# Another seven-product form for the second matrix product of an attention-and-GELU block

## The chip, the cores and the metric

The kernel runs on one core of a Trainium2 chip. The core has five engines with a queue of instructions each, worked through in order: TensorE (PE: matmuls, and PEld: the loads of their left sides), VectorE (DVE), ScalarE (ACT), GpSimd (POOL) and SyncE (SP, which only issues DMAs here). Engines wait for each other by semaphores. Matmul results lie in PSUM, in which the kernel holds eight tiles of 2 KB per partition (called banks here); everything else lies in SBUF. GpSimd does not read PSUM in this kernel.

The metric is the device time of one execution in microseconds. Before the change it is 203.3 us (median of three runs, 203.26 to 203.94).

## The reference

```python
# x: (8, 8, 512, 64), state: (8, 8, 32, 64): batches, heads, rows, depth
scores = scale * x @ state^T;   a  = softmax(scores);   xread = a  @ state
scores2 = scale * state @ x^T;  a2 = softmax(scores2);  sread = a2 @ x
rows = concatenate([xread, sread], axis=2)   # 8 batches of 512 + 32 rows, 512 wide
h = rows @ w_in                              # w_in: 512 x 2048
g = gelu(h)                                  # exact
out = g @ w_out                              # w_out: 2048 x 512, 4352 rows out
```

Inputs and output are float32; the kernel multiplies in bf16 and accumulates in float32.

## The kernel before, in words

For each of the eight batches the kernel makes the softmax weights `a`, folds the state into w_in (`P`, helpers `p_mm` and `p_all`), and gets g by `mm1`: two matmuls into a PSUM tile `hp` and one gelu on ScalarE, sixteen times per batch, written `M(k, k + 1)` for two of them. The 32 state rows of all batches together ("read-out") go through their own first product (`SR`) and second product (`R`).

The second product, g @ w_out, is plain for batch 0 (`mm2`). For batches 1 to 7 it is done in a seven-product form: g of a batch is cut into four quadrants `g_q(b, h, k)` (h: half of the rows, k: half of the 2048 inner columns), w_out into four quadrants `w_q[k][n]` (k: half of its rows, n: half of its columns). Seven products of quadrant size replace eight. Each left side is a quadrant of g or a sum of two (`g_sum`, one VectorE instruction of 128x2048 bf16, five per batch); each right side is a quadrant of w_out or a sum of two (`w_sums`, five in all, made once). A product is 16 matmuls (`x_mm`), and it accumulates in one of four banks `xp`. Products that share a bank are added there for free; the rest of the combination is done by `X` behind each product: per batch three bank copies on ScalarE, four adds on VectorE that read PSUM, and two subtractions on GpSimd (`u` and `v`, lines 658 and 622) of values in SBUF. The first product in a bank ("3" in bank 0) is copied before the second ("5") accumulates on it.

The order of the instructions is written out by hand; no scheduler moves them. From line 1171 on a loop runs over b, the batch whose g is being made, in eight slots p. Each slot begins with `M`, and most end with a product of batch b - 1. Slot 1 opens with the score matmuls of the next batch, slots 2 and 3 have its normalisation on VectorE (`norm`: a reduce, a reciprocal, a multiply), slot 5 has `p_all` (its matmuls use the banks of `xp` too) and then the first product of batch b itself, slot 7 the second. GpSimd rearranges the x of later batches (`rearr`, `rearr_ones`, lines 225 and 235) in slots 0, 5 and 7. SP's queue holds the output stores of the products (`x_out`) and the transposing DMAs of `xT` (slot 3) and `AT` (slot 5).

In the last pass (b = 7) slots 0 to 4 are `read_out_slot`: there the products of batch 6 stand between those of `SR`, which is a small seven-product form of its own, with adds on VectorE and ScalarE copies, in four PSUM tiles `sp` ("7" of it accumulates in the tile of "1", which VectorE reads in between). Slots 5 to 7 hold the products `R` of the read-out rows. Behind the loop come the products of batch 7, the last two of them in three pieces each (`l_mm`), so that adds and stores of the first pieces run beside the matmuls of the later ones.

The bank of each product, and the products that open one ("3" and "4" take a quadrant of g as it is):

```python
bank = {"3": 0, "4": 1, "5": 0, "2": 1, "1": 2, "6": 3, "7": 2}[name]
first = name in "3416"
```

Of the kernel before, what the change touches and what calls it, by code (L numbers as in the profile page):

```python
# [17 lines left out]
def kernel(  # L18
# [541 lines left out]
    w_sum = {}  # L560

    def w_add(name, x, y, op):
        if name == "3":
            pair = persist.tile([128, 2, MH, NH], BF16, name="ws_34", tag="mix0")
            w_sum["3"], w_sum["4"] = pair[:, 0], pair[:, 1]
        elif name != "4":
            tag = {"6": "mix1", "1": "mix2", "7": "mix3"}[name]
            w_sum[name] = persist.tile([128, MH, NH], BF16, name=f"ws_{name}", tag=tag)
        nc.vector.tensor_tensor(out=w_sum[name], in0=x, in1=y, op=op)

    def w_sums(i):
        (b11, b12), (b21, b22) = w_q
        w_add(*(
            ("3", b12, b22, ALU.subtract),
            ("4", b21, b11, ALU.subtract),
            ("6", b11, b12, ALU.add),
            ("1", b11, b22, ALU.add),
            ("7", b21, b22, ALU.add),
        )[i])
# [14 lines left out]
    def g_sum(b, name):  # L594
        (h0, k0), (h1, k1), op = G_SUMS[name]
        t = apool.tile([128, MH, 256], BF16, name="gsum", tag="gsum")
        nc.vector.tensor_tensor(out=t, in0=g_q(b, h0, k0), in1=g_q(b, h1, k1), op=op)  # L597
        xs[b, "g" + name] = t
# [20 lines left out]
    def c22(b):  # L619
        xs[b, "v"] = c_tile("v")  # L620
        o = xs[b, "o", 1]
        nc.gpsimd.tensor_tensor(  # L622
            out=xs[b, "v"], in0=xs[b, "q"], in1=o[:, :, :NH], op=ALU.subtract
        )
        if b < B - 2:
            c22_add(b)

    def c22_add(b):
        o = xs[b, "o", 1]
        nc.vector.tensor_tensor(out=o[:, :, NH:], in0=xs[b, 3], in1=xs[b, "v"], op=ALU.add)  # L630
        x_out(b, 1)

    def X(b, name):
        bank = {"3": 0, "4": 1, "5": 0, "2": 1, "1": 2, "6": 3, "7": 2}[name]
        first = name in "3416"
        if first:
            xs[b, bank] = otile([128, 2, NH], "xp", bank)
        ps = xs[b, bank]
        lhs = {"3": (0, 0), "4": (1, 1)}.get(name)
        lhs = xs[b, "g" + name] if lhs is None else g_q(b, *lhs)  # L640
        rhs = {"5": w_q[1][1], "2": w_q[0][0]}.get(name)
        rhs = w_sum[name] if rhs is None else rhs
        x_mm(ps, lhs, rhs, first)
        if name == "3":
            xs[b, "s3"] = c_tile("s3")
            if b > 1:
                nc.scalar.copy(out=xs[b, "s3"], in_=ps)
            for h in range(2):
                xs[b, "o", h] = hpool.tile([128, 2, d_model], FP32, name="oh", tag=f"oh{h}")
        elif name == "4":  # L650
            xs[b, "s34"] = c_tile("s34")
            nc.vector.tensor_tensor(out=xs[b, "s34"], in0=ps, in1=xs[b, "s3"], op=ALU.add)
        elif name == "5":
            o = xs[b, "o", 0][:, :, NH:]
            nc.scalar.copy(out=o, in_=ps)  # L655
            xs[b, "u"] = c_tile("u")
            x_out(b, 0, right)
            nc.gpsimd.tensor_tensor(out=xs[b, "u"], in0=xs[b, "s34"], in1=o, op=ALU.subtract)  # L658
        elif name == "2":
            nc.scalar.copy(out=xs[b, "o", 1][:, :, :NH], in_=ps)  # L660
            c22(b)
        elif name == "1":
            xs[b, "q"] = c_tile("q")
            nc.vector.tensor_tensor(out=xs[b, "q"], in0=ps, in1=xs[b, "s34"], op=ALU.add)
        elif name == "7":
            nc.vector.tensor_tensor(
                out=xs[b, "o", 0][:, :, :NH], in0=ps, in1=xs[b, "u"], op=ALU.add
            )
            x_out(b, 0, left)
# [8 lines left out]
    both = slice(0, 2)  # L678

    def L4():  # L680
        b = B - 1
        ps = xs[b, 1] = otile([128, 2, NH], "xp", 1)
        x_mm(ps, g_q(b, 1, 1), w_sum["4"], True)
        xs[b, "s34"] = c_tile("s34")
        nc.vector.tensor_tensor(out=xs[b, "s34"], in0=ps, in1=xs[b, "s3"], op=ALU.add)
        xs[b, "y"] = c_tile("q")
        nc.vector.tensor_tensor(out=xs[b, "y"], in0=xs[b, 3], in1=xs[b, "s34"], op=ALU.add)

    def L5():
        b = B - 1  # L690
        x_mm(xs[b, 0], xs[b, "g5"], w_q[1][1], False)
        nc.scalar.copy(out=xs[b, "o", 0][:, :, right], in_=xs[b, 0])
        rows_out(0, both, right, nc.sync)

    def L5_u():
        b = B - 1
        xs[b, "u"] = c_tile("u")
        nc.vector.tensor_tensor(
            out=xs[b, "u"], in0=xs[b, "s34"], in1=xs[b, "o", 0][:, :, right], op=ALU.subtract
        )  # L700

    def L2():
        b = B - 1
        x_mm(xs[b, 1], xs[b, "g2"], w_q[0][0], False)
        c21 = xs[b, "o", 1][:, :, left]
        nc.scalar.copy(out=c21, in_=xs[b, 1])
        rows_out(1, both, left, nc.sync)
        xs[b, "v"] = c_tile("v")
        nc.vector.tensor_tensor(out=xs[b, "v"], in0=xs[b, "y"], in1=c21, op=ALU.subtract)

    PIECES = ((0, 0, NH, 2), (1, 0, NH // 2, 0), (1, NH // 2, NH, 1))

    def l_mm(ps, name, j, n0, n1, first):
        for m in range(MH):
            nc.tensor.matmul(  # L715
                ps,
                lhsT=xs[B - 1, "g" + name][:, m, 128 * j:128 * j + 128],
                rhs=w_sum[name][:, m, n0:n1],
                start=(first and m == 0),
                stop=(m == MH - 1),  # L720
                skip_group_check=True,
            )

    def L1():
        b = B - 1
        for j, n0, n1, at in PIECES:
            ps = xs[b, "x", j, n0] = otile([128, n1 - n0], "xp", at)
            l_mm(ps, "1", j, n0, n1, True)
            nc.vector.tensor_tensor(
                out=xs[b, "o", 1][:, j, NH + n0:NH + n1],  # L730
                in0=ps,
                in1=xs[b, "v"][:, j, n0:n1],
                op=ALU.add,
            )
        rows_out(1, both, right, nc.sync)

    def L7():
        b = B - 1
        for j, n0, n1, at in PIECES:
            ps = xs[b, "x", j, n0]  # L740
            l_mm(ps, "7", j, n0, n1, False)
            nc.vector.tensor_tensor(
                out=xs[b, "o", 0][:, j, n0:n1], in0=ps, in1=xs[b, "u"][:, j, n0:n1], op=ALU.add
            )
            rows_out(0, slice(j, j + 1), slice(n0, n1), nc.scalar if n0 else nc.sync)
# [97 lines left out]
    def r_homes():  # L843
        pair = [att.tile([128, 2, MH, 128], BF16, name="rs", tag="xT") for _ in range(2)]
        one = att.tile([128, MH, 128], BF16, name="rs1", tag="AT")
        homes = [pair[0][:, 0], pair[0][:, 1], pair[1][:, 0], pair[1][:, 1], one]
        rs["homes"] = dict(zip("51267", homes))

    def r_sum(name):
        t = rs["g" + name] = rs["homes"][name]  # L850
        (h0, k0), (h1, k1), op = G_SUMS[name]
        nc.vector.tensor_tensor(out=t, in0=r_q(h0, k0), in1=r_q(h1, k1), op=op)
# [7 lines left out]
    def R(name):  # L860
# [4 lines left out]
        bank = {"3": 0, "4": 1, "5": 0, "2": 1, "1": 2, "6": 3, "7": 2}[name]  # L865
        first = name in "3416"
        if first:
            home = {"3": 1, "4": 2, "6": 2}
            rs[bank] = otile([128, NH], "rp", home[name]) if name in home else ftile([128, NH], "rp")
        ps = rs[bank]  # L870
        lhs = {"3": (0, 0), "4": (1, 1)}.get(name)
        lhs = rs["g" + name] if lhs is None else r_q(*lhs)
        rhs = {"5": w_q[1][1], "2": w_q[0][0]}.get(name)
        rhs = w_sum[name] if rhs is None else rhs
# [9 lines left out]
        add, sub = ALU.add, ALU.subtract  # L884
        if name == "3":
            nc.scalar.copy(out=c_new("s3"), in_=ps)
            for h in range(2):
                rs["o", h] = opool.tile([128, d_model], FP32, name="osb", tag="osb")
        elif name == "4":
            nc.vector.tensor_tensor(out=c_new("s34"), in0=ps, in1=rs["s3"], op=add)  # L890
        elif name == "5":
            o = rs["o", 0][:, NH:]
            nc.scalar.copy(out=o, in_=ps)
            nc.vector.tensor_tensor(out=c_new("u"), in0=rs["s34"], in1=o, op=sub)
        elif name == "1":
# [10 lines left out]
        elif name == "7":  # L906
            nc.vector.tensor_tensor(out=rs["o", 0][:, :NH], in0=ps, in1=rs["u"], op=add)
            r_out(0)
# [379 lines left out]
```

## Time and profile before

| what | us |
|---|---|
| median of three runs | 203.3 |
| profiled execution, whole time | 203.97 |
| its span, first to last instruction | 202.1 |
| TensorE matmul busy | 195.0 |
| VectorE busy | 155.9 |
| ScalarE busy | 139.2 |
| GpSimd busy | 67.3 |
| one product, 16 matmuls, in the chain | 1.75 |
| `g_sum` (L597), mean of 35 / median | 1.367 / 1.218 |
| add from PSUM, 128x512 float32 (L652, L664, L666, L630) | 0.68 to 0.69 |
| ScalarE bank copy, 128x512 (L647, L655, L660) | 0.59 |
| GpSimd `u` (L658), `v` (L622), mean | 1.47, 1.38 |

All durations are from one execution. The span is 1.87 us shorter than the whole time of that execution, and that execution is 0.67 us above the median. A timeline row has its start, its length, the engine and line, the operation with output and inputs, and in brackets the idle time of the engine before it and who ended it. Rows merged as x16 have the sum of their time. Lines are those of the program before.

### The profile page before, as it was taken

How to read it: one execution, taken by the hardware profiler on the slowest of the kernel's cores; microseconds unless marked ns; L12 is line 12 of the kernel's file. 1: busy time of each engine (PE TensorE's matmuls, PEld its weight loads, DVE VectorE, ACT ScalarE, POOL GpSimd, SP SyncE). 2: the span in 40 equal slices, each digit the busy share in tenths (PEclk: the TensorE clock that was granted, in tenths of full speed). 3: DMA queues.
4: the chain of work that ended last, by engine and by line, in shares of the span. 5: the costliest groups of instructions: out<-in, count | busy, mean ns of one | idle time of the engine just before them, and what ended most of it. 6: DMA issues, size and time to landing. Idle time of an engine off the chain costs nothing.

```text
span 202.1 us, 4900 instructions
## 1 busy us (share of the span) xinstructions
PE 195.0 (97%) x2030; PEld 134.4 (66%) x2035; DVE 155.9 (77%) x248; ACT 139.2 (69%) x251; POOL 67.3 (33%) x75
## 2 busy tenths in 40 slices
PE   7899999999999999999999999999999999999992
PEld 2434544465767677667767587677776878878892
DVE  2954875989996799986996967587758888894982
ACT  3785578798986878677967596688859477854020
POOL 8963503424259198431537202410220011200000
PEclk9999999999999999999999999999999999999999
DMA  6999999969665789592875208450107001040135
GB/s 195 196 171 203 205 199 194 181 140 158 89 116 107 208 96 156 116 133 78 107 156 148 63 2 112 146 114 0 52 27 184 3 0 55 0 159 0 52 105 159
DMA packets 40566, 23.16 MB, mean 115 GB/s; under 512 B 21856, under 2 KB 39136, under 8 KB 40544
## 3 DMA queue, kind: packets, MB, share of 16 engines
q0 software_dynamic: 13984, 8.10, 29.4%
q1 hardware_dynamic: 25872, 14.36, 29.3%
q10 hardware_dynamic: 688, 0.39, 0.6%
q8 instruction: 16, 0.26, 0.5%
q14 instruction: 6, 0.05, 0.1%
HBM read 17.30 MB, written 8.91 MB: 130 GB/s over the span
## 4 chain that ended last, share of the span: by engine, by line
PE 91%; DVE 5%; ACT 2%; issue 1%; ACTq 0%
PE xp L603 40%; PE hp L506 26%; PE op L548 5%; PE sp L810 3%; PE rp L876 3%; PE p_ps L441 2%; PE op L532 2%; PE xp L715 2%; PE pt L333 2%; PE warm_ps L150 2%; PE sr L917 1%; ACT P L955 1%; DVE gsum L597 1%; DVE P L955 1%; PE hp L1064 1%
## 5 line engine op out<-in xcount | busy, mean ns | idle before, releaser
L513 ACT ACTIVATE g<-hp 128x512 bf16<-128x512 f32 x124 | 65.9, 607 | 21.1 <-PE hp L506 14.8
L506 PE MATMUL hp<-AT,P 128*128 128x512 bf16 x248 | 61.2, 379 | 0.0
L603 PEld LDWEIGHTS <-gsum 128*128 128x128 bf16 x528 | 51.2, 98 | 11.4 <-DVE gsum L597 0.8
L597 DVE TENSOR_TENSOR gsum<-g 128x2048 bf16<-128x2048 bf16 x35 | 47.3, 1367 | 0.5
L506 PEld LDWEIGHTS <-P 128*128 128x128 bf16 x248 | 23.5, 98 | 20.6 <-issue 0.6
L603 PE MATMUL xp<-ws,gsum 128*128 128x256 bf16 x304 | 36.3, 273 | 0.4 <-DVE gsum L597 0.4
L603 PE MATMUL xp<-ws,g 128*128 128x256 bf16 x224 | 26.7, 272 | 0.3
L603 PE MATMUL xp<-w_out_bf,gsum 128*128 128x256 bf16 x224 | 26.6, 273 | 0.0
L603 PEld LDWEIGHTS <-g 128*128 128x128 bf16 x224 | 21.7, 98 | 5.3 <-issue 1.9
L658 POOL TENSOR_TENSOR u<-s,oh 128x512 f32<-128x512 f32 x6 | 8.8, 1468 | 40.1 <-ACT oh L655 40.1
L225 POOL COPY x<-xb 128x1024 bf16<-128x1024 bf16 x12 | 14.6, 1244 | 17.5 <-DMA xb<-in_x_dram 17.5
L622 POOL TENSOR_TENSOR v<-q,oh 128x512 f32<-128x512 f32 x6 | 8.3, 1379 | 19.5 <-ACT oh L660 17.2
L235 POOL COPY xo<-xb 128x1024 bf16<-128x1024 bf16 x12 | 12.1, 1041 | 5.0 <-PE sr L917 5.0
L955 ACT CAST P<-p_ps 128x512 bf16<-128x512 f32 x25 | 12.7, 606 | 0.1
L356 DVE TENSOR_TENSOR a<-e,ics 128x512 bf16<-128x512 bf16 x14 | 11.7, 834 | 0.5
L548 PE MATMUL op<-w_out_bf,g 128*128 128x512 bf16 x44 | 11.1, 380 | 0.5 <-issue 0.3
L955 DVE CAST P<-p_ps 128x512 bf16<-128x512 f32 x15 | 9.4, 684 | 1.7 <-PE p_ps L441 1.7
L353 DVE TENSOR_REDUCE cs<-e 128x16 f32<-128x512 bf16 x14 | 9.5, 677 | 0.9 <-ACT e L340 0.9
L441 PE MATMUL p_ps<-w_in_bf,sbd 64*32 64x512 bf16 x248 | 9.4, 380 | 0.0
L513 ACT ACT_TABLE_LOAD x7 | 9.0, 1283 | 0.1
L548 PEld LDWEIGHTS <-g 128*128 128x128 bf16 x48 | 4.2, 98 | 5.6 <-issue 0.8
L340 ACT ACT_TABLE_LOAD x6 | 7.7, 1283 | 0.1
(143 smaller groups left out, 240.7 us busy)
## 6 DMA issues: line engine op xcount, KB each, us to landing
out_dram<-oh SPq DMA_DIRECT2D x15, 256.0 KB, 2.5
xb<-in_x_dram POOLq DMA_DIRECT2D x7, 512.0 KB, 5.9
out_dram<-oh SPq DMA_DIRECT2D x6, 512.0 KB, 3.5
w_in_bf<-in_moe_w_in_dram POOLq DMA_DIRECT2D x6, 256.0 KB, 12.2
out_dram<-osb SPq DMA_DIRECT2D x5, 256.0 KB, 3.2
w_out_bf<-in_moe_w_out_dram POOLq DMA_DIRECT2D x4, 256.0 KB, 8.6
w_out_bf<-in_moe_w_out_dram POOLq DMA_DIRECT2D x2, 512.0 KB, 13.5
x0f<-in_x_dram SPq DMA_DIRECT2D x3, 256.0 KB, 3.9
```

The source lines that it names most:

```text
L225: nc.gpsimd.tensor_copy(out=A.x4[:, :, :, 64 * t:64 * t + 64].rearrange("p j c d -> p c j d"), in_=src[:, t],)
L235: eng.tensor_copy(out=A.xo[:, :, :, 2 + 64 * t:66 + 64 * t].rearrange("p j c d -> p c j d"), in_=src[:, t],)
L353: nc.vector.reduce_sum(out=cs, in_=e4, axis=AX.X)
L356: nc.vector.tensor_tensor(out=A.a[:, :, hs].rearrange("p g (c n) -> p g c n", n=NS), in0=e4, in1=ics[:, :, :].to_broadcast((128, G, 2, NS) ...
L441: nc.tensor.matmul(ps[t][32 * c:32 * c + 32, :], lhsT=sbd[64 * t:64 * t + 64, b, c, 32 * t:32 * t + 32], rhs=w_in_bf[64 * t:64 * t + 64, c ...
L506: nc.tensor.matmul(hp, lhsT=Ps[b][:, t, m * 128:(m + 1) * 128], rhs=atts[b].AT[:, :, t, :], start=(t == 0), stop=(t == 1),)
L513: nc.scalar.activation(out=gs[b][:, m, :], in_=hp, func=AF.Gelu)
L548: nc.tensor.matmul(ops[b, j], lhsT=gs[b][:, m, j * 128:(j + 1) * 128], rhs=w_out_bf[:, m, :], start=(m == 0), stop=(m == MC - 1),)
L597: nc.vector.tensor_tensor(out=t, in0=g_q(b, h0, k0), in1=g_q(b, h1, k1), op=op)
L603: nc.tensor.matmul(ps[:, j - js[0], :], lhsT=lhs[:, m, 128 * j:128 * j + 128], rhs=rhs[:, m, :], start=(first and j == js[0] and m == 0), ...
L658: nc.gpsimd.tensor_tensor(out=xs[b, "u"], in0=xs[b, "s34"], in1=o, op=ALU.subtract)
L955: copy(out=Ps[b][:, t, f * 512:(f + 1) * 512], in_=ps[t])
```

## The change

The seven products are those of another scheme. Its left sides are chained: "5" is a sum of two quadrants, "6" is "5" less a third, "3" is a quadrant less "6", and "7" is a difference by itself. So there are four sums per batch in place of five, and the products "1", "2" and "4" take quadrants as they are. The right sides are chained in the same way: four sums of w_out in place of five, `w_diff`. The products "1", "6" and "7" accumulate in one bank one after another, "5" and "3" in a second, "2" and "4" have one each. Per batch ScalarE copies four banks (`snap`: c2, c4, u, s5) and VectorE makes four adds, each of a bank and a copy; GpSimd has no part in it.

The order in the slots is new as well. Before: "4", "5", "1", "2" in slots 0 to 3, "7" in slot 5, and "3" and "6" of the batch itself in slots 5 and 7. After: "1", "6", "5", "7" in slots 0 to 3, "3" in slot 5, "2" and "4" of the batch itself in slots 5 and 7. The sums "5" and "6" are made together in slot 0, "7" in slot 2, "3" in slot 3. `sr_w`, which makes the sums for the read-out, moves from slot 0 to slot 1, behind product "6". In the read-out slots and in `R` the same scheme is used. Behind the loop the order is "1", "5" (in pieces), "6", `R("3")`, "7", "3" (in pieces); the lower half of the output rows of batch 7 leaves in one store of 512 KB after "7", the right half of the upper rows in three pieces after "3", where before there were stores of 256 KB after "5", "2" and "1" and three pieces after "7".

```diff
+    (b21, b22), (b11, b12) = w_q
+    def w_diff(name):
...
+        x, y = {
+            "5": (b12, b11),
+            "6": (b22, w_t.get("5")),
+            "7": (b22, b12),
+            "4": (b21, w_t.get("6")),
+        }[name]
+        nc.vector.tensor_tensor(out=w_t[name], in0=x, in1=y, op=ALU.subtract)
...
+    def chain(name, q, got):
+        a11, a12, a21, a22 = q(0, 1), q(0, 0), q(1, 1), q(1, 0)
+        return {
+            "1": (a11,),
+            "2": (a12,),
+            "4": (a22,),
+            "5": (a21, a22, ALU.add),
+            "6": (got.get("5"), a11, ALU.subtract),
+            "7": (a11, a21, ALU.subtract),
+            "3": (a12, got.get("6"), ALU.subtract),
+        }[name]
...
+    BANK = {"2": 0, "1": 1, "6": 1, "7": 1, "5": 2, "3": 2, "4": 3}
+
+    def add(out, x, y):
+        nc.vector.tensor_tensor(out=out, in0=x, in1=y, op=ALU.add)
+
+    def snap(b, name, tag, ps):
+        xs[b, name] = c_tile(tag)
+        nc.scalar.copy(out=xs[b, name], in_=ps)
...
+        x_mm(ps, x_lhs(b, name), w_rhs(name), first)
+        if name == "2":
             if b > 1:
-                nc.scalar.copy(out=xs[b, "s3"], in_=ps)
+                snap(b, "c2", "c2", ps)
+        elif name == "4":
+            snap(b, "c4", "c4", ps)
+        elif name == "1":
...
+            add(xs[b, "o", 0][:, :, left], ps, xs[b, "c2"])
+            x_out(b, 0, left)
+        elif name == "6":
+            snap(b, "u", "u", ps)
         elif name == "5":
...
+            snap(b, "s5", "s5", ps)
+        elif name == "7":
+            add(xs[b, "o", 1][:, :, right], ps, xs[b, "s5"])
+            add(xs[b, "o", 1][:, :, left], ps, xs[b, "c4"])
+            x_out(b, 1)
+        elif name == "3":
+            add(xs[b, "o", 0][:, :, right], ps, xs[b, "u"])
             x_out(b, 0, right)
-            nc.gpsimd.tensor_tensor(out=xs[b, "u"], in0=xs[b, "s34"], in1=o, op=ALU.subtract)
...
+            if p < 5 and nb < B:
                 if p == 0:
-                    g_sum(b - 1, "5")
-                    if b > 2:
-                        sr_w("5216"[b - 3])
-                X(b - 1, "45127"[p])
-                if p < 3:
-                    g_sum(b - 1, "127"[p])
+                    g_sum(b - 1, "56")
+                if p == 2:
+                    g_sum(b - 1, "7")
+                if p == 3:
+                    g_sum(b - 1, "3")
+                if p < 4:
+                    X(b - 1, "1657"[p])
+                if p == 1 and b > 2:
+                    sr_w("5216"[b - 3])
...
@@ read_out_slot
             SR("5", 1)
             SR("2", 1)
             SR_gelu("52", 1)
-            X(c, "2")
+            X(c, "7")
             SR("1", 1)
             SR("6", 1)
         if p == 4:
             M(k, k + 1)
             SR_gelu("6", 1)
             SR("7", 1)
             SR_gelu("7", 1)
-            c22_add(c)
-            X(c, "7")
+            X(c, "3")
...
             if p == 5:
-                X(b - 1, "7")
+                X(b - 1, "3")
...
-                g_sum(b, "6")
...
-                X(b, "3")
+                X(b, "2")
...
-                X(b, "6")
+                X(b, "4")
     b = B - 1
-    for name in "521":
-        g_sum(b, name)
-    L4()
-    g_sum(b, "7")
+    g_sum(b, "56")
+    X(b, "1")
+    g_sum(b, "73")
     L5()
-    L5_u()
-    L2()
-    R("7")
-    L1()
-    L7()
+    X(b, "6")
+    R("3")
+    X(b, "7")
+    L3()
```

## The prediction

> **What bounds the kernel now.** I read the page first, then the waits of TensorE, a table by stretch, and then the timeline at those places where the change puts a wait in front of TensorE. The page's chain that ended last, and the waits:
>
> ```profile
> span 202.1 us, 4900 instructions
> PE 195.0 (97%) x2030; PEld 134.4 (66%) x2035; DVE 155.9 (77%) x248; ACT 139.2 (69%) x251; POOL 67.3 (33%) x75
> PE 91%; DVE 5%; ACT 2%; issue 1%; ACTq 0%
> ...
> PE xp L603 <- DVE gsum L597: 0.4, 1, 0.4
> ...
> 42.00:198.00 156.00, 155.26 (x1660) 115.98 (x1657) 127.92 (x182) 110.76 (x201) 45.74 (x42) 1.00 0.46 93
> ```
>
> The reader should see that from 42 to 198 us, where all seven-product work lies, TensorE is busy 155.26 of 156.00 us at the full clock (the last line: length, then busy time of PE, PEld, DVE, ACT, POOL). It waits for VectorE's sums once, 0.4 us. So TensorE's queue sets the time: every added microsecond of TensorE waiting is a microsecond of the kernel, and work taken from VectorE, ScalarE or GpSimd gains only where TensorE waited for it.
>
> The Trainium skill ("Perfetto Trace Analysis", Identifying the Most-Contended Engine) says that matmul busy time is a poor measure and that weight-load busy time should be used for TensorE's headroom. By that reading VectorE (77%) stands above TensorE's weight loads (66%), and the 8.5 us of sums taken from VectorE would be a gain of up to 8.5 us. The chain (91% PE) and the 0.4 us of waits speak against it here.
>
> **The change part by part.** The profiled execution took 203.97 us, 1.87 us more than its span; the median of the runs is 203.3, so 0.67 lower. I add the terms to the span and carry the sum over to the median.
>
> Matmuls: the listings of both programs have the same number of TensorE instructions, each product still 16 matmuls in 1.75 us. Cost 0.
>
> VectorE in all: one sum less in each of seven batches (7 x 1.218, the median of L597) and one w sum less (1.2 at 29.7 us). In 42 to 198 TensorE waited 0.42 us for a sum, before the product with g_sum "6" of batch 4; that product now is "4", with a raw left side, so 0.42 goes (between 0 and 0.42). What is late next there is the transpose of srm that stands ahead of it, which did not wait. GpSimd: twelve subtractions (17.1 us) go; those who waited for them were VectorE's L630 (4.7 us) and no TensorE row, so 0. ScalarE: one copy of 0.59 more per batch; the new one, "c4", comes after slot 7, where ScalarE idled 1.4 to 2.0 us before the next gelu; if that cover were gone it would delay a gelu by 0.59 and TensorE by no more than that. Output DMAs of the loop: SP's count is the same but x_out(b, 1) now leaves in slot 3 after two adds, about 1.5 us earlier than L630 allowed, ahead of the transposing DMA of slot 5 that is queued behind it; 0.
>
> The new waits. Product "6" now accumulates in the bank whose value after "1" VectorE must first add to c2 (0.69), and this add is queued behind the chained sums "5" and "6" (2 x 1.22). Between "1" and "6" TensorE has only the scores and two mm1 (1.2 us).
>
> Batch 1 (loop pass b=2). A P cast stands ahead on VectorE:
>
> ```profile
> 51.44 1.92 PE L603 MATMUL xp<-ws,g 128*128 128x256 bf16 x16
> 51.61 0.69 DVE L453 CAST P<-p_ps 128x512 bf16<-128x512 f32 x1
> 52.22 1.22 DVE L597 TENSOR_TENSOR gsum<-g 128x2048 bf16<-128x2048 bf16 x1
> ...
> 54.53 1.91 PE L603 MATMUL xp<-w_out_bf,gsum 128*128 128x256 bf16 x16
> ```
>
> The second product of this pass is due at 54.53 and needed one sum, ready at 53.44. Now: 52.22 + 1.22 + 1.22 = 54.70 with the gaps, the add until 55.4, product "6" at 55.47. **+0.94** (0.9 without gaps; 1.4 if both sums take 1.45 as the one at 60.08 does).
>
> Batch 2 (b=3). Here GpSimd's copies stand in the way of the first sum:
>
> ```profile
> 71.62 3.16 DVE L597 TENSOR_TENSOR gsum<-g 128x2048 bf16<-128x2048 bf16 x1
> 71.67 2.03 POOL L235 COPY xo<-xb 128x1024 bf16<-128x1024 bf16 x2
> ...
> 76.25 1.91 PE L603 MATMUL xp<-w_out_bf,gsum 128*128 128x256 bf16 x16
> ...
> 76.51 3.19 DVE L597 TENSOR_TENSOR gsum<-g 128x2048 bf16<-128x2048 bf16 x2
> 76.65 3.94 POOL L225 COPY x<-xb 128x1024 bf16<-128x1024 bf16 x2 [1.01 <-DMA xb<-in_x_dram]
> ```
>
> The sum took 3.16 instead of 1.22 and ended at 74.78. The chained one ends at 76.0, the add at 76.7, and "6" starts at 76.77 instead of 76.25: **+0.5** (0 if the sum gets ahead of the copies, 1.3 if the second one is slowed as well by what GpSimd does at 73.7 to 75.6). Then sr_w, now behind that add, meets the next copies: blocked from 76.65 to 78.7, sr_w until 79.96, norm 1.7, sum "7" until 82.9, while product "7" is due at 82.2 with the 0.5 counted. That is 0.75 if GpSimd comes first, as the 0.1 us between the two rows has it, and 0 if VectorE does: I take **+0.4**.
>
> Batches 3 to 5: from 92.83 the sums end at 95.3; "1" ends at 96.29, its add at 97.02, "6" is due at 97.46. 0.4 us to spare, and the same at 118.8 and 140.0; 0. Product "7" of batch 3 has 0.2 to spare by the same working.
>
> Batch 6, in the read-out slots, where VectorE also makes the adds of the small seven-product form:
>
> ```profile
> 170.36 0.69 DVE L831 TENSOR_TENSOR srt<-sp,srt 128x512 f32<-128x512 f32 x1 [0.43 <-ACT srt L821]
> 170.97 1.22 DVE L597 TENSOR_TENSOR gsum<-g 128x2048 bf16<-128x2048 bf16 x1
> ...
> 172.16 0.69 DVE L824 TENSOR_TENSOR srt<-srt 128x512 f32<-128x512 f32 x1
> 172.96 0.69 DVE L827 TENSOR_TENSOR srt<-srt 128x512 f32<-128x512 f32 x1
> ...
> 174.08 1.49 DVE L831 TENSOR_TENSOR srt<-sp,srt 128x512 f32<-128x512 f32 x2 [0.44 <-PE sp L810]
> ...
> 175.19 0.61 PE L810 MATMUL sp<-srx,srw 128*128 128x128 bf16 x8
> ```
>
> SR("7", 1) at 175.19 needs the first of the two adds at 174.08. In the new queue the two adds of X "7" stand before them. From 170.48, with the gaps: 0.69, sum 1.22, 0.69, 0.69, then 2 x 0.69, then 0.69: 176.1, so SR("7", 1) starts at 176.15. **+0.95** (0.7 without gaps, 1.05 at most). The first pass, SR("7", 0), has 0.1 to spare: 0.
>
> The end. After the last gelu VectorE makes "5" and "6" (until 190.5), the add after "1" (191.4), "7" and "3" (193.8), each before TensorE needs it (190.5, 192.2, 194.8, 196.6), and the copy "u" (194.78) before 194.82: no wait. But the last store grows:
>
> ```profile
> 194.82 3.70 PE L715 MATMUL xp<-ws,gsum 128*128 128x256 bf16 x48
> ...
> 197.11 1.91 SPq L674 DMA_DIRECT2D out_dram<-oh  x3
> 197.66 0.74 DVE L742 TENSOR_TENSOR oh<-xp,u 128x256 f32<-128x256 f32 x2 [0.58 <-PE xp L715]
> 198.56 0.29 DVE L742 TENSOR_TENSOR oh<-xp,u 128x128 f32<-128x128 f32 x1 [0.15 <-PE xp L715]
> 198.88 0.37 ACTq L674 DMA_DIRECT2D out_dram<-oh  x1
> ```
>
> Now, 256 KB leave at 197.11 and 256 KB in pieces until 198.88; the table by stretch has the last bytes at 200.1 and the span ends at 202.1, 2.0 later. After the change "7" ends at 196.73, its two adds at 198.16, and one store of 512 KB leaves at 198.2. The pieces' adds follow at 198.6, 198.9 and 199.2. From issue to first bytes 0.85 (the body's 512 KB, issued at 107.81, flow from about 108.6), then 768 KB at 350 to 400 KB/us, as in 199 to 200: last bytes at 201.0, so **+0.9** (0.35 if only the last issue counts; 1.3 at 330 KB/us).
>
> The Trainium skill ("DMA: Bandwidth & Descriptors", Anatomy of one DMA) gives 2.0 us plus bytes at 436 KB/us for a transfer, fitted on GpSimd's path. Applied to each store by itself, the 64 KB issued last at 199.2 would set the end and the term would be 0.35; the stores that overlap in the trace at 380 KB/us speak for a shared rate and 0.9.
>
> Sum: 0.94 + 0.5 + 0.4 + 0.95 + 0.9 - 0.42 = 3.27. Span 205.4, profiled execution 207.2, median 206.6.
>
> **Rivals.** *More waits than counted* (VectorE sets slots 1 to 3): the 0.4 and 0.2 us to spare in batches 3 to 5 are used up by GpSimd's copies, as at 71.62. Against it: from batch 4 on GpSimd is done with its copies before the sums. Three batches at 0.5 each: +1.5, 208.1.
>
> *Only the end grows*: the sums and adds arrive in time, since VectorE has less to do. For it: 127.92 busy of 156. Against it: the queues above. A wait of one batch and the end: 0.9 + 0.5 - 0.42, or 1.0: 204.3. Without any wait 0.48: 203.8, within 0.5% of no change.
>
> *Faster*: the relief of GpSimd. Without its subtractions the sums that were slowed run at 1.22; L597 averages 1.367 over 35, so 5.2 us lie in that. If the chain's pieces of VectorE and ScalarE around the P casts (about 0.6 us in each of five passes) were behind such slowed work, 5 x 0.6 less the end's 0.9 gives -2.1: 201.2. It decides if "6" in pass b=2 starts at 54.5. Against it: those pieces are ScalarE's casts of p_ps, which wait for matmuls, and the slow sums lie beside copies that stay.
>
> **How the numbers follow.** The forecast as summed 0.58; more waits 0.18; only the end grows 0.17, of which 0.07 within what a measurement can tell; faster 0.07. What a measurement of this kernel can tell from no change is about 0.5%, 1.0 us. The low ends of the terms give 203.3 + 0.9 + 0 + 0 + 0.7 + 0.35 - 0.42 = 204.8, the high ends 203.3 + 1.4 + 1.3 + 0.75 + 1.05 + 1.3 = 209.1. With a tenth left out on each side, where one more term may vanish below: 204.3 to 208.3. Faster 0.07, same 0.07, slower 0.58 + 0.18 + 0.10, or 0.86.
>
> **What would show it.** In the profile after: TensorE's xp rows wait for VectorE's oh or gsum about 1 us in pass b=2 and 0.5 to 1.2 us in b=3; an sp row waits about 0.9 us for srt near 176; no sum waits in batch 4; VectorE's last add stands about 0.35 us further behind TensorE's last matmul, and the span ends about 3.8 us behind that add, where it now ends 3.25 behind it. If those waits are absent, or the last store flows before 198, the prediction is wrong.

## The result, and the profile after

The changed kernel takes 205.39 us (median of six runs, 205.29 to 206.05) against 203.62 for the kernel before measured beside it (six runs, 203.18 to 204.26). The ratio is 1.0092, with a 95% interval of 1.0066 to 1.0117: slower by 0.9%. The profiled execution took 205.37 us with a span of 203.6, 1.5 us more than the span of before. Ratios leave out executions in a slower state, with a lower granted clock; of all those below that is one, of 206.50 us at a clock of 0.983.

The page of the changed kernel, with the rows of TensorE's waits for VectorE and the table by stretch:

```profile
span 203.6 us, 4865 instructions
PE 195.5 (96%) x2035; PEld 133.9 (66%) x2035; DVE 142.7 (70%) x233; ACT 143.3 (70%) x261; POOL 51.5 (25%) x63
...
PE xp L623 <- DVE oh L642: 0.9, 2, 0.7
PE sp L781 <- DVE srt L802: 0.2, 1, 0.2
...
42.00:198.00 156.00, 154.55 (x1643) 114.96 (x1640) 114.21 (x166) 114.87 (x211) 29.32 (x30) 1.00 0.47 91
```

VectorE has 13 us less to do than before, GpSimd 16 us less, and the kernel is slower. TensorE has the same matmuls (2035 records of them here and 2030 before; a trace lacks a few), and between 42 and 198 us it is now idle for 1.45 us where it was idle for 0.74. The new waits are for `oh` (the adds out of a bank) and for `srt` (an add of the read-out); the wait for a sum is gone.

The first wait, in the timeline of pass b=2 (start, length, engine and line, operation):

```profile
51.46 0.69 DVE L453 CAST P<-p_ps 128x512 bf16<-128x512 f32 x1 [1.41 <-PE p_ps L441]
52.07 1.21 DVE L613 TENSOR_TENSOR gsum<-g 128x2048 bf16<-128x2048 bf16 x1
53.32 1.23 DVE L613 TENSOR_TENSOR gsum<-gsum,g 128x2048 bf16<-128x2048 bf16 x1
54.46 0.68 DVE L642 TENSOR_TENSOR oh<-xp,c 128x512 f32<-128x512 f32 x1
55.20 1.91 PE L623 MATMUL xp<-ws,gsum 128*128 128x256 bf16 x16 [0.65 <-DVE oh L642]
```

The add that frees the bank of "1" for "6" stands behind both chained sums, and these behind a cast for which VectorE itself had waited 1.41 us. TensorE was through with everything else at 54.55 and waits for the end of that add.

The second, in pass b=3:

```profile
72.28 3.13 DVE L613 TENSOR_TENSOR gsum<-g 128x2048 bf16<-128x2048 bf16 x1
72.30 2.03 POOL L235 COPY xo<-xb 128x1024 bf16<-128x1024 bf16 x2
...
75.45 1.23 DVE L613 TENSOR_TENSOR gsum<-gsum,g 128x2048 bf16<-128x2048 bf16 x1
76.59 0.68 DVE L642 TENSOR_TENSOR oh<-xp,c 128x512 f32<-128x512 f32 x1
77.19 2.12 DVE L741 TENSOR_TENSOR srw<-w_in_bf 128x1024 bf16<-128x1024 bf16 x2
77.21 3.01 POOL L225 COPY x<-xb 128x1024 bf16<-128x1024 bf16 x2 [0.93 <-DMA xb<-in_x_dram]
77.33 1.91 PE L623 MATMUL xp<-ws,gsum 128*128 128x256 bf16 x16 [0.25 <-DVE oh L642]
```

The first sum again took 3.13 us in place of 1.22 beside GpSimd's copies, though its row starts 0.02 us ahead of theirs. Below it the two sums `srw` start 0.02 us ahead of the next copies, and here the first of them runs at its usual 0.68 us, while the copy beside it takes 1.57 and the second sum 1.53. They end at 79.3; "7" of this batch did not wait.

The read-out, and then the end (its table by stretch gives the length, five engines' busy time, the clock, the DMA share and the GB/s), with two rows of the same table of the kernel before below it:

```profile
174.11 0.69 DVE L642 TENSOR_TENSOR oh<-xp,s 128x512 f32<-128x512 f32 x1
174.72 0.68 DVE L642 TENSOR_TENSOR oh<-xp,c 128x512 f32<-128x512 f32 x1
175.32 1.48 DVE L802 TENSOR_TENSOR srt<-sp,srt 128x512 f32<-128x512 f32 x2
176.05 0.61 PE L781 MATMUL sp<-srx,srw 128*128 128x128 bf16 x8 [0.22 <-DVE srt L802]
```

```profile
200.00:200.50 0.50, 0.00 (x0) 0.00 (x0) 0.00 (x0) 0.00 (x0) 0.00 (x0) 1.00 1.02 410
...
201.50:202.00 0.50, 0.00 (x0) 0.00 (x0) 0.00 (x0) 0.00 (x0) 0.00 (x0) 1.00 0.97 283
```

```profile
200.00:200.50 0.50, 0.00 (x0) 0.00 (x0) 0.00 (x0) 0.00 (x0) 0.00 (x0) 1.00 0.11 34
200.50:201.00 0.50, 0.00 (x0) 0.00 (x0) 0.00 (x0) 0.00 (x0) 0.00 (x0) 1.00 0.03 9
```

VectorE's rows start 0.60 us apart though each lasts 0.68. The last bytes leave at about 201.9. Before, the main flow ended at about 200.1, but 34 and then 9 GB/s went on behind it, in steps of 0.1 us until about 200.7.

Together, as differences of the two traces (how much later each product starts than before, less what it was late already):

| place | predicted | measured |
|---|---|---|
| start (first of the seven products at 42.27, before at 42.42) | – | -0.15 |
| "6" in pass b=2 | +0.94 | +0.82 |
| "6" in pass b=3 | +0.5 | +0.41 |
| "7" in pass b=3 | +0.4 | 0 |
| passes b=4 to 6 | 0 | 0 |
| batch 4, wait for sum "6" | -0.42 | -0.59 |
| `SR("7", 1)` | +0.95 | +0.38 |
| last store | +0.9 | +0.64 |
| sum | 3.27 | 1.51 |

The sum of the measured column is the difference of the spans, 1.5 us.

### The profile page after: what moved, and what is told of

Same layout as the page of the kernel before. It is cut to its first block, busy times and chain, and to the rows that moved or that the text cites. A ratio compares the mean times of both kernels' runs of the same rounds, so it can differ in the third digit from the quotient of the medians.

```text
span 203.6 us, 4865 instructions
## 1 busy us (share of the span) xinstructions
PE 195.5 (96%) x2035; PEld 133.9 (66%) x2035; DVE 142.7 (70%) x233; ACT 143.3 (70%) x261; POOL 51.5 (25%) x63
## 4 chain that ended last, share of the span: by engine, by line
PE 84%; DVE 4%; DMA 4%; ACT 3%; issue 2%; DVEq 0%; POOL 0%; ACTq 0%; POOLq 0%
PE xp L623 38%; PE hp L506 24%; PE op L548 5%; PE rp L847 3%; PE sp L781 3%; DMA xb<-in_x_dram 3%; DVE oh L642 2%; PE p_ps L441 2%; PE op L532 2%; DMA st_f<-in_state_dram 2%; ACT P L915 1%; PE pt L333 1%; PE sr L877 1%; PE xp L694 1%; PE hp L1022 1%
## 5 line engine op out<-in xcount | busy, mean ns | idle before, releaser
L623 PEld LDWEIGHTS <-gsum 128*128 128x128 bf16 x416 | 40.4, 98 | 10.3 <-issue 1.2
L623 PEld LDWEIGHTS <-g 128*128 128x128 bf16 x336 | 32.4, 98 | 6.9 <-issue 1.9
L623 PE MATMUL xp<-w_out_bf,g 128*128 128x256 bf16 x224 | 26.7, 273 | 0.3
L613 DVE TENSOR_TENSOR gsum<-g 128x2048 bf16<-128x2048 bf16 x14 | 19.0, 1355 | 0.5
L646 ACT COPY c<-xp 128x512 f32<-128x512 f32 x14 | 8.3, 593 | 9.8 <-PE xp L623 4.5
L623 PE MATMUL xp<-ws,g 128*128 128x256 bf16 x112 | 13.4, 273 | 0.0
L642 DVE TENSOR_TENSOR oh<-xp,u 128x512 f32<-128x512 f32 (+2 forms) x9 | 5.0, 569 | 10.8 <-PE xp L623 10.8
L642 DVE TENSOR_TENSOR oh<-xp,c 128x512 f32<-128x512 f32 x14 | 9.6, 685 | 4.0 <-PE xp L623 4.0
L623 PE MATMUL xp<-w_out_bf,gsum 128*128 128x256 bf16 x96 | 11.5, 273 | 0.0
L613 DVE TENSOR_TENSOR gsum<-g,gsum 128x2048 bf16<-128x2048 bf16 x7 | 9.4, 1339 | 0.0
```

What stands on the lines that cost most here:

```text
L613: nc.vector.tensor_tensor(out=got[name], in0=x, in1=y, op=op)
L623: nc.tensor.matmul(ps[:, j - js[0], :], lhsT=lhs[:, m, 128 * j:128 * j + 128], rhs=rhs[:, m, :], start=(first and j == js[0] and m == 0), ...
L642: nc.vector.tensor_tensor(out=out, in0=x, in1=y, op=ALU.add)
L646: nc.scalar.copy(out=xs[b, name], in_=ps)
```

## Experiments

The code ahead of the first of the seven products is nearly the same in all kernels, yet in the profiles that product starts anywhere from 42.22 to 43.06 us. So profiles are compared by the time from that product, taken where the chain has it, to the end of the span: 159.68 us before, 161.33 after. Counted from there they repeat well: the runs with late adds in the read-out, with the last store in two and with one more sum start every product ahead of the place of their edit, and the last two all products, within 0.01 us of the changed kernel's. Medians of the whole time are given beside it; they hold the scatter of the start as well.

### "5" before "6"

```diff
-                    X(b - 1, "1657"[p])
+                    X(b - 1, "1567"[p])
```

> The changed kernel with products "5" and "6" exchanged in slots 1 and 2 of the loop (order "1", "5", "6", "7"); the read-out slots and the end stay. Theory A (TensorE waits for the chained sums and the add that stand ahead of "6" on VectorE, 0.82 us in pass b=2 and 0.41 in b=3): both waits go, no other comes, time 205.4 - 1.2 = 204.2, and the span's part from 50 to 80 us is shorter by 1.2. Rival B (the bank of "1", "6" and "7" is the limit, not the sums): "7" now follows "6" with only two mm1 between and waits for ScalarE's copy u instead, 0.2 to 0.5 us in each of five passes, so 204.5 to 206.5 and TensorE's xp rows wait for ScalarE's u. Rival C (those waits are not what the time went to): 205.4.

Measured: 204.72 us (ten runs; before 203.93 beside it), ratio 1.0054 (1.0026 to 1.0081); from the first product 161.01, 0.32 less than after. Both waits in front of "6" are gone, and no product waits for the copy `u`, the sign of rival B. The median is 0.5 above the 204.2 of theory A. The profiled execution, 205.33 us, has a new wait further on in pass b=2:

```profile
58.01 3.08 POOL L225 COPY x<-xb 128x1024 bf16<-128x1024 bf16 x2 [4.87 <-DMA xb<-in_x_dram]
58.13 2.06 DVE L613 TENSOR_TENSOR gsum<-g 128x2048 bf16<-128x2048 bf16 x1
62.54 2.06 DVE L613 TENSOR_TENSOR gsum<-g,gsum 128x2048 bf16<-128x2048 bf16 x1
64.66 1.92 PE L623 MATMUL xp<-w_out_bf,gsum 128*128 128x256 bf16 x16 [0.65 <-DVE gsum L613]
```

GpSimd's copies started 0.12 us ahead of the sum "7", which then took 2.06 us; the queue of VectorE stayed behind, and "3" waited 0.65 for its sum. Product "3" stands as far behind the first product as in the changed kernel (22.2 us), so the gain of 0.82 in this pass was given back whole in this execution; of the 0.41 of pass b=3, 0.33 is left at the read-out. The order of "6" and "5" was the cause of the two waits; taking them away uncovers the next queue on VectorE. The sum "7" starts behind GpSimd's copies, and takes 2.06 us, in the profiles of the next two experiments too, at no cost: there "6" is still 0.82 late, and TensorE comes to "3" that much later. By the medians this run gained more than its profile shows: its ratio is 1.0054 against 1.0092, some 0.8 us.

### The adds of "7" behind the read-out's products

```diff
-            X(c, "7")
+            X(c, "7", late=True)
             SR("1", 1)
             SR("6", 1)
+            X7_out(c)
```

`late=True` leaves out the two adds and the store behind the product, and `X7_out`, a new function, holds them.

> The changed kernel with the two adds and the store behind product "7" of batch 6 issued after SR("1", 1) and SR("6", 1) in the read-out slots; nothing else differs. Theory A: the small product SR("7", 1) no longer waits for VectorE, 0.38 us less, 205.0; later VectorE work has room there. Rival (another instruction of VectorE, the sum "3", holds the adds of SR back anyhow): the wait of the sp row stays at 0.2 or more, and the span is the same within 0.1 us.

Measured: 205.57 us (one run), from the first product 160.92, 0.41 less than after. The row of the read-out's wait is gone, and the read-out's adds on VectorE now wait for TensorE:

```profile
175.16 1.49 DVE L805 TENSOR_TENSOR srt<-sp,srt 128x512 f32<-128x512 f32 x2 [0.43 <-PE sp L784]
```

The two adds of X "7" ahead of the read-out's own adds were what `SR("7", 1)` waited for, and their price was 0.4: it starts 0.38 earlier, and everything ahead of it within 0.01. The whole time, 205.57, missed the 205.0 expected, since the first product started 0.61 later in this execution than in the changed kernel's.

### The last store in two

```diff
             add(xs[b, "o", 1][:, :, right], ps, xs[b, "s5"])
+            if b == B - 1:
+                x_out(b, 1, right)
             add(xs[b, "o", 1][:, :, left], ps, xs[b, "c4"])
-            x_out(b, 1)
+            x_out(b, 1, left if b == B - 1 else slice(None))
```

> The changed kernel with the last 512 KB store of batch 7 cut in two: the right half leaves after the first add behind "7", the left half after the second. Theory A (the bytes that are still to be sent when TensorE has done set the end: 0.64 us of the difference): 256 KB start 0.6 us earlier, so the last bytes come 0.3 to 0.6 us earlier, 204.8 to 205.1. Rival (the last small piece's own issue and landing set the end, whatever is sent before it): 205.4. Second rival (shorter runs of 1 KB in place of 4 KB, and one more issue on SP, cost what the earlier start gives): 205.4 or up to 0.4 more.

Measured: 205.40 us (six runs), ratio 1.0068 (1.0045 to 1.0091); from the first product 160.92. The stores and the last adds:

```profile
198.11 0.69 DVE L642 TENSOR_TENSOR oh<-xp,s 128x512 f32<-128x512 f32 x1 [1.38 <-PE xp L623]
198.83 0.97 SPq L637 DMA_DIRECT2D out_dram<-oh  x2
199.32 0.81 DVE L642 TENSOR_TENSOR oh<-xp,u 128x256 f32<-128x256 f32 x3
```

The span ends 3.47 us behind the end of the last add (200.13), where it ended 3.88 behind it in the changed kernel; up to that add all products and adds stand where they stood. So the first half, which now leaves 0.7 us behind the start of the first add and not 1.3, gives back 0.4 us, all of it at the end, as theory A had it. It repeats: in the six profiles of the changed kernel and its versions without this edit the span ends 3.8 to 3.9 us behind the last add, in the three with it 3.4 to 3.5. The medians alone (205.40 and 205.39, ratios 1.0068 and 1.0092 with intervals that overlap) do not tell this run from the changed kernel, and the expected 204.8 to 205.1 was missed.

### All three

The three edits above in one kernel.

> All three edits together in the changed kernel: "5" before "6" in the loop, late adds in the read-out, the split last store. Theory A: 205.4 - 1.2 - 0.4 - 0.4 = 203.4, the time of the kernel before within what can be told; what is left against it is the end, 0.2 us longer, against 0.6 us that the raw quadrant of "4" takes off in batch 4. Rival B: 204 to 206, with waits for ScalarE's copy u.

Measured: 204.44 us (twelve runs, 203.62 to 205.29), ratio 1.0020 (1.0000 to 1.0041); from the first product 159.34, 0.34 less than the kernel before and 1.99 less than after. No product and no matmul of the read-out waits for VectorE in this profile. In pass b=2 GpSimd's copies and the sum "7" came in the other order:

```profile
58.59 1.22 DVE L613 TENSOR_TENSOR gsum<-g 128x2048 bf16<-128x2048 bf16 x1
58.69 3.01 POOL L225 COPY x<-xb 128x1024 bf16<-128x1024 bf16 x2 [5.10 <-DMA xb<-in_x_dram]
```

Here the sum is 0.10 us ahead of the copies and takes 1.22, and "3" does not wait; that is the difference to the first experiment. The gains stand at their places: 1.2 by pass b=3, 0.38 at `SR("7", 1)`, 0.4 at the end. So the three places account for the loss: without them the scheme of the changed kernel costs nothing that the profile shows against the old one. By the medians it is still 0.5 us longer than the kernel before, and the 203.4 expected was missed by 1.0. Part of that may be the start, which stands at 43.06 in this profile and at 42.42 before, part the sum "7" in other executions; the experiment on w_out "7" is about that.

### One more sum per pass on VectorE

```diff
+            if p == 4 and nb < B:
+                t = apool.tile([128, MH, 256], BF16, name="gidle", tag="gidle", bufs=1)
+                nc.vector.tensor_tensor(out=t, in0=g_q(b - 1, 0, 0), in1=g_q(b - 1, 1, 1), op=ALU.add)
```

> The changed kernel with one more sum per pass on VectorE, 128x2048 bf16, whose result nothing reads: in slot 4 of passes b=2 to 6 (batches 1 to 5). It gives VectorE back 5 x 1.22 = 6.1 us of work. Theory (TensorE's queue sets the time, VectorE's load is worth nothing away from the waits): the span behind the first product stays at 161.3 us, within 0.3, the ratio to the kernel before stays near 1.009. Rival (VectorE is near its limit, so that its relief was a gain hidden behind the new waits): +1.2 us per pass, up to 6 us, 211.

Measured: 205.73 us (ten runs; before 203.88 beside it), ratio 1.0082 (1.0057 to 1.0107); from the first product 161.28, against 161.33. The stretch from 42 to 198:

```profile
42.00:198.00 156.00, 154.55 (x1641) 115.00 (x1638) 119.85 (x171) 114.83 (x211) 28.76 (x29) 1.00 0.45 90
```

VectorE is busy 5.6 us longer and TensorE is busy as long as in the changed kernel, to the hundredth; every product starts within 0.01 us of where it stood. VectorE's load is worth nothing in this slot, since it makes nothing late that TensorE waits for; what counts is what stands ahead of the few awaited instructions.

### GpSimd's subtractions back

```diff
             snap(b, "s5", "s5", ps)
+            if b < B - 1:
+                t = c_tile("idle")
+                nc.gpsimd.tensor_tensor(out=t, in0=xs[b, "u"], in1=xs[b, "s5"], op=ALU.subtract)
...
             x_out(b, 1)
+            if b < B - 1:
+                t = c_tile("idle")
+                nc.gpsimd.tensor_tensor(out=t, in0=xs[b, "c4"], in1=xs[b, "s5"], op=ALU.subtract)
```

> The changed kernel with two unused GpSimd subtractions of 128x512 float32 per batch again (batches 1 to 6, behind products "5" and "7"; nothing reads the results), as the kernel before had them: 12 x 1.4 = 17 us of GpSimd work. Theory (nobody on TensorE's path waited for GpSimd's subtractions): span behind the first product 161.3 within 0.5, since the copies of x may move against the sums by a few tenths. Rival (the relief of GpSimd is a gain that hides part of the cost): 1 to 2.1 us longer, 206.5 to 207.5.

Measured: 208.44 us (four runs, 207.79 to 208.99), ratio 1.0207 (1.0162 to 1.0252); from the first product 164.10, 2.77 more than after, and more than the rival's 206.5 to 207.5. The theory falls. The place in pass b=4:

```profile
106.28 1.59 POOL L678 TENSOR_TENSOR idle<-c,s 128x512 f32<-128x512 f32 x1
...
106.67 2.28 DVE L613 TENSOR_TENSOR gsum<-g,gsum 128x2048 bf16<-128x2048 bf16 x1
...
109.01 1.92 PE L623 MATMUL xp<-w_out_bf,gsum 128*128 128x256 bf16 x16 [0.49 <-DVE gsum L613]
```

Neither instruction reads what the other writes, and nobody reads the subtraction's result; yet the sum "3" beside it takes 2.28 us, and TensorE waits. Product "3" loses 0.48, 0.66 and 0.67 in passes b=2 to 4 and nothing in b=5 and 6, and `SR("7", 1)` loses 1.07: there an add of the read-out took 1.76 us in place of 0.69 beside a subtraction of 2.15. The sum in pass b=4 became 1.06 us longer and TensorE lost 0.67, so the sum had 0.4 us to spare there. In pass b=2 the sum "7" also started behind the copies of x (2.06 us), so the 0.48 there is not shown to be the subtractions' alone; passes b=3 and 4 are clear of that.

Two things stay open. Both subtractions run in a row in slots 2 and 3 here, since the second needs only the copies; the kernel before had them apart, behind "5" and behind "2". Two runs that would settle this, the changed kernel with each subtraction at a place of its own and the kernel before without its subtractions, were set up and gave no result. So 2.8 us is the price of these subtractions at these places, and not of GpSimd's work in general. For the kernel before the trace says this much: of its 35 sums one lies beside a subtraction (at 60.08, 1.45 us), and no product waited for it.

### The sum of w_out "7" before the loop

The version with all three edits, and:

```diff
     X(1, "4")
+    w_diff("7")
...
-            if b == 2 and p == 1:
-                w_diff("7")
```

> The version with all three repairs ("5" before "6", late adds in the read-out, the last store in halves), with the sum of w_out "7" made before the loop, where VectorE idles 1.4 us, and no longer in slot 1 of pass b=2. Theory: VectorE is 1.2 us earlier in slot 2 of that pass, so the sum "7" at 58.1 to 58.6 always starts ahead of GpSimd's copies and the race that cost 0.65 in one profile is gone: median 203.6 to 204.0, against 204.4 with the three repairs alone. Rival (the race is won in most executions anyway, and what is left over the kernel before is scatter or another cause): no difference from 204.4.

Measured: 204.08 us (twelve runs, 203.41 to 206.50; before 203.88), ratio 1.0001 (0.9973 to 1.0029); from the first product 159.35. The sum "7" of pass b=2 is now well ahead of the copies:

```profile
57.05 1.22 DVE L613 TENSOR_TENSOR gsum<-g 128x2048 bf16<-128x2048 bf16 x1
...
58.30 2.48 POOL L225 COPY x<-xb 128x1024 bf16<-128x1024 bf16 x2 [5.11 <-DMA xb<-in_x_dram]
```

It starts 1.25 us before them. By the medians alone the two theories are not told apart: 204.08 lies between them, and the interval holds both. The spans say more. With all three edits the twelve spans run from 201.8 to 203.5, median 202.55, two of them at or below 202.0, and the kernel before, run beside it, had a median of 202.0. Now eight of the eleven that enter the ratio lie between 201.6 and 202.0, median 201.8, with 201.9 for the kernel before. That fits a sum that came behind the copies in part of the executions and now always comes ahead of them, but the two were not run beside each other, and it is not shown. This version equals the kernel before within what can be measured, and no kernel here beats that one.

### The P cast on ScalarE

```diff
-                pmat(2, 2)
+                p_copy_s(2, 2, p_mm(2, 2, ftile))
```

> The changed kernel with one cast of P (batch 2, fourth quarter) on ScalarE in place of VectorE, where it stood ahead of the sums "5" and "6" of pass b=2. Theory (product "6" waits there because the two sums and the add are queued behind that cast): the sums start 0.6 to 0.7 us earlier, the wait of 0.9 before "6" in pass b=2 falls to 0.2 to 0.3, span behind the first product 160.7. Rival (the wait is for the product "1" or for the ScalarE copy c2 and not for the queue of VectorE): the wait stays at 0.9, or grows as ScalarE is later with its copies.

Measured: 204.77 us (one run), from the first product 160.44, 0.89 less than after. Pass b=2:

```profile
51.53 1.22 DVE L613 TENSOR_TENSOR gsum<-gsum,g 128x2048 bf16<-128x2048 bf16 x1
53.51 0.69 DVE L642 TENSOR_TENSOR oh<-xp,c 128x512 f32<-128x512 f32 x1 [0.75 <-PE xp L623]
54.57 1.91 PE L623 MATMUL xp<-ws,gsum 128*128 128x256 bf16 x16
```

The sums, which had stood behind the cast, are done at 52.75, VectorE idles 0.75 until "1" is done, and "6" does not wait at all: 12.27 us behind the start of the first product's row in place of 13.09. The expectation left a wait of 0.2 to 0.3; it was right in the cause and cautious in the size, because the sums came forward by 2.0 us against the first product and not by 0.7: with the cast went VectorE's own wait for the matmuls that the cast reads.

## Why the prediction was right, and where it was not

It said slower, 206.6 us with a range of 204.3 to 208.3; 205.39 is slower and within it. The places where TensorE would wait were right, with one exception, but their sum was twice too large: by spans it counted 3.27 us and 1.5 came. The forecast lies 1.2 us above the measured time; from the 203.62 that the kernel before took beside it, and not the 203.3 it started from, it would have been 1.5. No term came out above its forecast, and only the width of the range took that up. Its steps, in its order:

- *TensorE's queue sets the time, work taken from others gains only where TensorE waited.* Right: the fifth sum put back cost nothing, while three places of some tenths each carry the loss that the profiles show. The Trainium skill's measure ("Perfetto Trace Analysis", Identifying the Most-Contended Engine), by which VectorE would have stood above TensorE, does not agree with these traces: the kernel with 13 us less VectorE work is the slower one, and 5.6 us put back cost nothing.
- *Product "6" in pass b=2, +0.94.* Right, 0.82. The swap and the cast on ScalarE each took the wait away, so both causes named, the sums ahead of the add and the cast ahead of the sums, are shown. Most of the 0.1 too much is that the add starts 0.09 before the second sum's row ends.
- *Product "6" in b=3, +0.5.* Right, 0.41; the first sum took 3.13 us beside the copies as predicted.
- *Product "7" in b=3, +0.4.* Not there. This was near the mean of two outcomes, 0 and 0.75, that the working left open, with its rows speaking for the 0.75: that 0 came was luck. The sums `srw` were slowed by the copies only in their second half and ended at 79.3, where 79.96 had been counted. That the order of such a pair can decide is shown at 58 us, where "3" waited in the first run and not in the fourth.
- *Batches 3 to 5, 0.* Right: no wait in three passes.
- *`SR("7", 1)`, +0.95.* The place and the cause were right, the size was not: 0.38. The step counted each VectorE row with its length of 0.69 and a gap, though rows that follow each other at once start 0.60 us apart. The rows of before already showed it (170.36 and 170.97 for one of 0.69), and the step passed over it; it also began its count at 170.48, 0.12 behind that row.
- *The end, +0.9.* 0.64. That the larger last store costs something is shown by its cut in two, which gave back 0.4. The sum went by bytes, and these came when it said: with TensorE 0.86 later, the last at 201.9 stand for its 201.0. But it counted 2.0 us from the last bytes of before, at 200.1, to the end of the span, and 1.7 came: what it had read as the last bytes was the end of the main flow, and a trickle went on until about 200.7. What sets the time from the last bytes to the end of the span stays open. Of its signs, the last add stands no further behind TensorE than before, where 0.35 was expected: again the spacing of VectorE's rows. The 3.8 us from that add to the end of the span were right (3.88). The Trainium skill's sum for one transfer ("DMA: Bandwidth & Descriptors", Anatomy of one DMA), applied to each store by itself, had given an estimate of 0.35, which is too low here; the stores overlap and share 283 to 410 GB/s from 200.0 to 202.0.
- *The wait for the sum in batch 4, -0.42.* -0.59: the product followed the transpose ahead of it by 0.64 us before and by 0.05 after. The bracket of 0.42 counted only the idle time behind the transpose's row of 0.22 us.
- *GpSimd's subtractions go, 0.* As a difference between the two kernels it held, as far as the two traces show: TensorE's only wait for a sum before was beside copies of x, which stayed, and the table leaves nothing over. But the step's reason, that no TensorE row waited for the subtractions, looked only at who reads their results. Put into the new order they cost 2.8 us by slowing sums and adds that they have nothing to do with, so the 0 came out right by where the subtractions stood before, which is luck as far as the step goes.

Of the rivals, *more waits than counted* did not come: batches 3 to 5 have their tenths to spare, as long as GpSimd is quiet. *Only the end grows* falls by the two waits in front of "6". *Faster* named its point, "6" in pass b=2 at 54.5; it started at 55.20, with TensorE 0.15 ahead of before.

## What to carry to other kernels

Where one engine's queue sets the time, price a change by what stands ahead of each awaited instruction in the queue that releases it, and not by the busy time that it saves: here 13 us less work on VectorE gained nothing, and one add of 0.7 us behind two sums cost 0.8. Take the spacing of back-to-back rows from the trace, not their lengths. When rows of two engines that slow each other start within 0.1 us, carry both outcomes through the sum with a chance for each and not their mean, and give the awaited one a microsecond of lead where the queue has an idle place further up.

## What was not expected of the hardware

- VectorE's float32 adds of 128x512 last 0.68 to 0.69 us in the profile but start 0.60 to 0.61 apart when they follow each other (174.11, 174.72, 175.32).
- A 128x2048 sum took 1.22 us when it started 0.10 to 0.15 us ahead of a GpSimd copy of 128x1024 (58 us, three profiles), and the copy 1.96 to 2.02 in place of 1.05; it took 2.06 when it started 0.07 to 0.13 behind (four profiles). Closer than that, the order of the rows does not tell who is slowed: at 72.28 the sum stands 0.02 ahead of two copies and takes 3.13, while they take their usual 1.05 each, and at 77.19 a sum 0.02 ahead runs at its usual length and the copy takes 1.57. GpSimd pays in subtractions too: one of 1.26 us took up to 2.15.
- The first of the seven products started between 42.22 and 43.06 us in ten profiles, with nearly the same instructions ahead of it. That is half of what the whole change costs, and so single times say little here. From that product on the starts of products repeat within 0.01 us between profiles of like kernels.
